# Narrower token tables in a fused attention and mixture-of-experts kernel, with the compact list read back from DRAM

## The chip, the cores and the metric

The kernel runs on one core of a Trainium2 chip. What counts is the device time of one execution in microseconds (us). Three runs of the kernel before took 1440.1, 1440.43 and 1440.45 us; the median is 1440.43.

## What is computed

Linear attention without a softmax feeds a mixture of experts that picks one expert per token; its rows feed a dense layer with a cosine.

```python
kv  = einsum('bhsd,bhse->bhde', k, v)            # 8 batches, 8 heads, 576 rows, 64 columns
out = einsum('bhsd,bhde->bhse', q, kv)
x   = out / sqrt(mean(out*out) + 1e-6) * g_norm   # as 4608 tokens of 512

e   = argmax(x @ w_gate)                          # one of 8 experts per token
y   = softmax(x @ w_gate)[e] * (relu(x @ w1[e]) @ w2[e])   # 512 -> 1024 -> 512

h   = y @ w_in                                    # 512 -> 2048
o   = (h * cos(h)) @ w_out                        # 2048 -> 512
```

Which token goes to which expert is known only on the chip, so the kernel keeps tables of token numbers.

## The kernel before

Everything is one function, `fused_kernel`, in which each engine's instructions stand in the order in which the Python code emits them; no scheduler moves them. An engine runs its own stream in order and waits on semaphores for the others.

**Attention and routing.** For each of the 8 batches TensorE makes `kv` (`emit_kv`), transposes q (`emit_qT`) and multiplies (`emit_out`), five row blocks `j` per batch. The VectorE work of the batch before is a generator, `route(b)`, from which `pump` takes three steps at a time between the TensorE calls: norms, logits, the expert's one-hot `esel`, the token's rank within its expert `rsel`. The rank is split into a row `cc` (rank modulo 128) and a column `aa` (expert times 36, plus rank divided by 128). For each row block, `emit_hot` (L513) builds two one-hot matrices on VectorE, `oc` (128 columns) and `oa` (288 columns, 36 per expert, times the token's number), and `emit_list` (L523) adds `oc^T @ oa` into the PSUM tile `lst`: 40 matmuls in all, two batches behind the attention. The result, `ids[p, e, t]`, holds the number of the token of rank 128 t + p of expert e. Experts are taken in order of their counts (`emit_order`); `emit_idx(r, ...)` selects the first 6 of the 36 columns of the r-th of them into `idx`, by which `gather` fetches token rows (GpSimd's indirect DMA).

**First layer of experts (moe1).** For each rank r of 8, `emit_f1` runs eight blocks c in one or two halves, and `emit_f2` four blocks in two halves, every product as three fp32r passes. `emit_f1` writes to one of three PSUM buffers, which ScalarE (L291) and VectorE (L292) empty; `emit_f2` and the transposes `emit_xT` of the next expert's rows share four PSUM buffers, and a transposed block is emptied by ScalarE (L272) and VectorE (L273). Between them stand, in this order, the split of one weight block into two parts (`next_split`, ScalarE with GpSimd L208 or VectorE L220), one step of the conversion of the dense layer's float64 weights (`prep`: VectorE L878 to L894, ScalarE L897 and L899, GpSimd L900 and L901), steps of `tables`, and `emit_clist`.

**Tables.** `tables` is a generator of VectorE operations, taken two steps per block of `emit_f1` and one per half of `emit_f2`. It makes the remaining `idx`, the counts, the first output column `basei` of each expert, the overflow counts `ovi`, and then for every token its position in the compact output: three times a product over 128x320 (L786) and its sum (L790), then `posq`, `posc`, `posa` (L795 to L806).

**The compact list.** `emit_clist` (L823) builds one-hots from those positions on VectorE (L835, L838) and adds them by matmul (L829) into the PSUM tile `clist`, one of 40 row blocks per half of `emit_f2` from r = 1 on. L1022 converts it into `ctok`, by which the dense layer's rows are scattered to the output (L1104).

**Overflow.** `emit_overflow` (L958) reads the overflow counts into registers of all engines (L960) and branches. No instruction behind that branch is in the trace.

**Dense layer (moe2).** Nine groups of 512 tokens by 16 blocks. Its weights come from the DRAM copy `wsp` by DMAs on GpSimd's queue (`load_m2`, L911).

SyncE issues the DMAs of q, k, v, of the attention rows `xs`, of the expert weights (L198, L213), of the raw dense weights and of the rows `ys` (L917), all in program order.

```python
def emit_list(b, j):
    oc, oa = tl.pop(("oh", b, j))
    nc.tensor.matmul(lst[:, 0:E * LT], lhsT=oc, rhs=oa, ...)
...
for u in range(2 * KD):
    if r > 0 or u % 2:
        emit_f2(r, u // 2, u % 2)
    next_split()
    prep()
    next(tabs, None)
    if r > 0:
        emit_clist()
    if r + 1 < E and u < ntile[r + 1]:
        emit_xT(r + 1, u)
```

Of the kernel before, what the change touches and what calls it, by code (L numbers as in the profile page):

```python
# [20 lines left out]
GATHER = 6  # L21
# [11 lines left out]
def fused_kernel(  # L33
# [43 lines left out]
    slots = dram.tile([(E + 1) * NT, 1], I32, name="slots")  # L77
    wsp = dram.tile([2 * C2, P, 2, 512], F32, name="wsp")
# [41 lines left out]
    def load_q(b):  # L120
        if b < B:
            load_rows(q[b], QT[b % 2])

# [10 lines left out]
    iota_a = const.tile([P, E * LT], F32, name="iota_a")  # L134
    nc.gpsimd.iota(iota_a, pattern=[[1, E * LT]], base=-E * LT, channel_multiplier=0,
                   allow_small_or_imprecise_dtypes=True)
    iota_b = const.tile([P, LT], F32, name="iota_b")
    nc.gpsimd.iota(iota_b, pattern=[[1, LT]], base=0, channel_multiplier=0,
# [44 lines left out]
    rsel = const.tile([P, B, NJ], F32, name="rsel")  # L183
    esel = const.tile([P, B, NJ, E], BF16, name="esel")
# [211 lines left out]
    def route(b):  # L396
# [39 lines left out]
        fm = sm([P, NJ], "fm")  # L436
        V.tensor_reduce(out=fm, in_=cd, axis=AX.X, op=ALU.min)
        tl["fm", b] = fm
# [34 lines left out]
        while ("rk", b) not in tl:  # L473
# [39 lines left out]
    def emit_hot(b, j):  # L513
# [4 lines left out]
        oa = late.tile([P, E * LT], F32R, tag="oa", name="oa", bufs=3)  # L518
# [64 lines left out]
    idx = const.tile([P, E, GATHER], I32, name="idx")  # L583

    def emit_idx(r, tab, sm=sm, n=GATHER):
# [3 lines left out]
        u = sm([P, GATHER], "iu")  # L589
# [5 lines left out]
    lst3 = lst[:, 0:E * LT].rearrange("p (e t) -> p e t", e=E)  # L595
    ids = const.tile([P, E, LT], F32, name="ids")
# [135 lines left out]
    basei = const.tile([P, E], I32, name="basei")  # L732
    ovi = const.tile([P, 2 * E + 1], I32, name="ovi")
    posc = const.tile([P, B * NJ], F32, name="posc")
    posa = const.tile([P, B * NJ], F32, name="posa")

    def tables(sm):
        V = nc.vector
        BT = B * NJ
# [6 lines left out]
        cols = sel.rearrange("p r e -> p e r")  # L746
# [27 lines left out]
        V.tensor_tensor(out=bov, in0=bov, in1=basef, op=ALU.subtract)  # L774
        V.tensor_tensor(out=bov, in0=bov, in1=capr, op=ALU.subtract)
        yield
# [3 lines left out]
        picks = []  # L780
        for n, vec in (("be", basef), ("de", bov), ("ce", capr)):
            ve = sm([P, E], n)
            rows(ve, cols, vec)
            yield
            t2 = sm([P, BT, E], "t2")
            V.tensor_tensor(out=t2, in0=esel.rearrange("p b j x -> p (b j) x"),  # L786
                            in1=ve[:, None, :].to_broadcast([P, BT, E]), op=ALU.mult)
            yield
            pk = sm([P, BT], "p" + n)
            V.tensor_reduce(out=pk, in_=t2, axis=AX.X, op=ALU.add)  # L790
            picks.append(pk)
            yield
        be, de, ce = picks
        rs = rsel.rearrange("p b j -> p (b j)")
        V.tensor_tensor(out=ce, in0=rs, in1=ce, op=ALU.is_ge)  # L795
        V.tensor_tensor(out=de, in0=de, in1=ce, op=ALU.mult)
        yield
# [25 lines left out]
    def emit_clist():  # L823
        i = len(hot2)
        if i > B * NJ + 1:
            return
# [346 lines left out]
```

## Time and profile before

| | us |
|---|---|
| median of three runs | 1440.43 |
| profiled execution, first to last instruction (span) | 1435.0 |
| what lies around the span (the difference of the two) | 5.4 |
| TensorE (PE) busy | 1370.3 (95%) |
| VectorE (DVE) busy | 976.2 (68%) |
| ScalarE (ACT) busy | 620.1 (43%) |
| GpSimd (POOL) busy | 389.5 (27%) |

The profile page gives no time of the profiled execution but its span. Attention lies at about 0 to 140 us, the first expert and the tables at 140 to 240, the rest of moe1 up to 632, the dense layer from 637 to the end. An engine's busy share is no measure of what bounds it; the waits of TensorE, and what ended each, say more. PEld is TensorE's weight load. A bracket in a timeline row, [4.00 <-DVE xreg L273], says how long the engine was idle before that row and which instruction released it.

### The profile page before, as it was taken

Reading aid. Unit: us, or ns where it says so; the run is one execution under the profiler, and the core shown is the slowest. Engines: PE = TensorE matmul, PEld = TensorE weight load, DVE = VectorE, ACT = ScalarE, POOL = GpSimd, SP = SyncE. Lnnn points to the kernel's source line nnn. Section 1 sums busy time; section 2 is a strip of 40 time slices with the busy share of each in tenths; the row PEclk is TensorE's granted clock in tenths of the full one; section 3 lists DMA queues with packets and bytes.
Section 4 is the critical chain, followed back from the end, with each engine's and each line's share of the span. In section 5 each row is a group of like instructions: output and inputs, shape, how many; then the busy total and the mean of one; then the engine's idle time right before and its main releaser. Section 6 shows DMA issues by size and latency. Waiting matters only on the chain.

```text
span 1435.0 us, 21374 instructions
## 1 busy us (share of the span) xinstructions
PE 1370.3 (95%) x8046; PEld 1208.8 (84%) x8046; DVE 976.2 (68%) x1720; ACT 620.1 (43%) x1195; POOL 389.5 (27%) x416
## 2 busy tenths in 40 slices
PE   6996798999999999989999999999999999999998
PEld 5885797999999999988888888888888888888886
DVE  2898868888888996316666666666666666665665
ACT  4886233444444444424434333443333433434333
POOL 1345534547456565220111101111011110011101
PEclk9998998999999999999999999999999999999999
DMA  9984355657676675774200001010000100000000
GB/s 316 340 295 136 129 151 170 213 186 219 201 220 209 196 240 167 221 223 148 88 30 23 22 16 30 30 30 30 8 23 30 30 30 15 16 30 1 30 0 30
DMA packets 137232, 162.22 MB, mean 113 GB/s; under 512 B 9428, under 2 KB 115924, under 8 KB 136096
## 3 DMA queue, kind: packets, MB, share of 16 engines
q1 hardware_dynamic: 111904, 97.54, 22.0%
q0 software_dynamic: 15296, 53.21, 10.9%
q10 hardware_dynamic: 9920, 10.03, 2.1%
q8 instruction: 65, 1.06, 0.3%
q14 instruction: 47, 0.39, 0.1%
HBM read 115.08 MB, written 45.66 MB: 112 GB/s over the span
## 4 chain that ended last, share of the span: by engine, by line
issue 32%; PE 18%; POOL 4%; DVE 1%; POOLq 0%; ACT 0%; DVEq 0%
PE gp L1046 9%; PE acc L1093 9%; POOL xreg L925 2%; POOL out_dram L1104 2%; DVE ra L1062 0%; DVE ra L1064 0%; DVE ni L1060 0%; POOL spare L1111 0%; POOLq L1168 0%; ACT ra L1067 0%; POOLq L925 0%; ACT ra L1066 0%; DVE ra L1074 0%; ACT gg L1075 0%; POOLq L1104 0%
## 5 line engine op out<-in xcount | busy, mean ns | idle before, releaser
L1046 PE MATMUL gp<-xreg,wA 128*128 128x512 f32 x1728 | 418.3, 392 | 5.2 <-ACTq L960 5.2
L1093 PE MATMUL acc<-wB,gg 128*128 128x512 f32 x1728 | 418.6, 391 | 0.1
L1046 PEld LDWEIGHTS gp<-xreg,wA 128*128 128x128 f32 x1728 | 325.9, 189 | 75.3 <-ACTq L960 5.5
L1093 PEld LDWEIGHTS acc<-wB,gg 128*128 128x128 f32 x1728 | 324.3, 188 | 70.8 <-DVE gg L1081 0.5
L1066 ACT ACTIVATE ra<-ra 128x512 f32<-128x512 f32 (+1 forms) x147 | 91.7, 623 | 380.6 <-DVE ra L1064 380.6
L289 PE MATMUL hp<-xreg,wA 128*128 128x352 f32 (+7 forms) x1536 | 226.1, 307 | 11.3 <-DVE wB L292 10.7
L289 PEld LDWEIGHTS hp<-xreg,wA 128*128 128x128 f32 x1536 | 219.0, 191 | 16.1 <-DVE wB L292 15.3
L302 PE MATMUL yp<-wB,wA 128*128 128x352 f32 (+7 forms) x1536 | 228.5, 307 | 4.1 <-DVE xreg L273 4.0
L302 PEld LDWEIGHTS yp<-wB,wA 128*128 128x128 f32 x1536 | 218.2, 190 | 4.6 <-DVE xreg L273 4.1
L1060 DVE TENSOR_SCALAR ni<-gp 128x512 int32<-128x512 f32 (+1 forms) x147 | 100.0, 680 | 170.3 <-PE gp L1046 170.3
L1074 DVE TENSOR_TENSOR ra<-gp,ra 128x512 f32<-128x512 f32 (+1 forms) x147 | 100.0, 680 | 114.8 <-ACT ra L1067 114.7
L925 POOL TENSOR_TENSOR xreg<-yst,xreg 128x512 fp32r<-128x512 f32 x32 | 41.5, 1296 | 367.3 <-ACT xreg L923 367.3
L1075 ACT ACTIVATE gg<-ra 128x512 fp32r<-128x512 f32 (+1 forms) x147 | 91.7, 624 | 92.8 <-DVE ra L1074 92.4
L1104 POOL DMA_INDIRECT out_dram<-oo,ctok x36 | 35.7, 993 | 331.3 <-DVE oo L1103 323.5
L1067 ACT ACTIVATE ra<-ra,half_pi 128x512 f32<-128x512 f32 (+1 forms) x147 | 105.1, 715 | 4.8
L1064 DVE SCALAR_TENSOR_TENSOR ra<-ni,ra 128x512 f32<-128x512 int32 (+1 forms) x147 | 100.1, 681 | 5.1
L208 POOL TENSOR_TENSOR wA<-w1s,wA 128x512 fp32r<-128x512 f32 x64 | 85.4, 1339 | 65.1 <-ACT wA L207 64.5
L1062 DVE SCALAR_TENSOR_TENSOR ra<-ni,gp 128x512 f32<-128x512 int32 (+1 forms) x147 | 99.5, 677 | 5.0
L1081 DVE TENSOR_TENSOR gg<-ra,gg 128x512 fp32r<-128x512 f32 (+1 forms) x147 | 98.9, 674 | 0.2 <-ACT gg L1075 0.2
L292 DVE SCALAR_TENSOR_TENSOR wB<-hp,wB 128x352 fp32r<-128x352 f32 (+7 forms) x128 | 57.7, 469 | 51.0 <-ACT wB L291 50.8
L291 ACT ACTIVATE wB<-hp 128x352 fp32r<-128x352 f32 (+7 forms) x128 | 52.6, 422 | 84.1 <-PE hp L289 83.7
L309 ACT ACTIVATE yo<-yp 128x352 f32<-128x352 f32 (+7 forms) x64 | 27.1, 423 | 89.7 <-PE yp L302 71.2
(188 smaller groups left out, 1308.9 us busy)
## 6 DMA issues: line engine op xcount, KB each, us to landing
w1s<-in_moe_w_dram SPq DMA_DIRECT2D x64, 256.0 KB, 4.4
w2s<-in_moe_w_dram SPq DMA_DIRECT2D x64, 256.0 KB, 3.7
wsp<-cd POOLq DMA_DIRECT2D x32, 512.0 KB, 4.0
yst<-ys SPq DMA_DIRECT2D x36, 256.0 KB, 2.6
xs<-xo SPq DMA_DIRECT2D x16, 512.0 KB, 4.3
raww<-in_moe_w_in_dram SPq DMA_DIRECT2D x16, 512.0 KB, 5.1
raww<-in_moe_w_out_dram SPq DMA_DIRECT2D x16, 512.0 KB, 5.2
wA<-wsp POOLq DMA_DIRECT2D x16, 512.0 KB, 5.2
```

Of the source, the lines that this page charges most:

```text
L289: nc.tensor.matmul(ps, lhsT=wv[:, a, kk, :], rhs=xT[:, b, kk, sl], start=(i == 0 and kk == 0), stop=(i == 2 and kk == KD - 1))
L302: nc.tensor.matmul(ps, lhsT=wv[:, a, kk % 4, :], rhs=hT[:, kk, b, sl], start=(n == 0), stop=(n == 3 * C1 - 1))
L1046: nc.tensor.matmul(ps, lhsT=wv[:, a, kk, :], rhs=yv[:, b, kk, :], start=(n == 0), stop=(n == 3 * KD - 1))
L1060: nc.vector.tensor_scalar(out=ni[:, h], in0=ps[:, h], scalar1=INV_2PI, scalar2=None, op0=ALU.mult)
L1062: nc.vector.scalar_tensor_tensor(out=ra[:, h], in0=ni[:, h], scalar=-PI2_HI, in1=ps[:, h], op0=ALU.mult, op1=ALU.add)
L1064: nc.vector.scalar_tensor_tensor(out=ra[:, h], in0=ni[:, h], scalar=-PI2_LO, in1=ra[:, h], op0=ALU.mult, op1=ALU.add)
L1066: nc.scalar.activation(ra[:, h], ra[:, h], AF.Abs)
L1067: nc.scalar.activation(ra[:, h], ra[:, h], AF.Sin, scale=-1.0, bias=half_pi)
L1074: nc.vector.tensor_tensor(out=ra[:, h], in0=ps[:, h], in1=ra[:, h], op=ALU.mult)
L1075: nc.scalar.activation(gg[:, 0, h], ra[:, h], AF.Copy)
L1081: nc.vector.tensor_tensor(out=gg[:, 1, h], in0=ra[:, h], in1=gg[:, 0, h], op=ALU.subtract)
L1093: nc.tensor.matmul(acc[g][t], lhsT=gg[:, a, t * P:(t + 1) * P], rhs=wv[:, b, :], start=(c == 0 and n == 0), stop=(c == C2 - 1 and n == 2))
```

## The change

Three parts.

1. The list's one-hot `oa`, the PSUM tile `lst` and `ids` have 6 columns per expert (48 in all) in place of 36 (288). A token of rank 768 or more gets a column outside the table: `route` has two more VectorE operations per batch, `qf` and an addition to `aa`.
2. `tables` loses the step between `ovi` and the remaining `idx`, and all that follows them (L780 to L806). Instead, `emit_idx` keeps its sums in `idf`, TensorE transposes it once (128x48 to 48x128, tile `idp`), and VectorE converts that into `idT`.
3. `emit_clist`, its 40 pairs of one-hots and 40 matmuls go. SyncE copies the 6 rows of `idT` of each expert into a DRAM list `cid` at that expert's first column, in the order of the experts, so that each copy overwrites the tail of the one before; after the branch one DMA reads `ctok` back from `cid`: 128 partitions by 36 single numbers of 4 bytes. SyncE therefore also loads `basei` into a register for seven experts. The code behind the overflow branch is rewritten to fit.

```diff
+    cid = dram.tile([2 * NT + P, 1], I32, name="cid")
...
-    iota_a = const.tile([P, E * LT], F32, name="iota_a")
+    iota_a = const.tile([P, E * GATHER], F32, name="iota_a")
...
+        qf = sm([P, NJ], "qf")
-        V.scalar_tensor_tensor(out=aa, in0=tl["fm", b], scalar=float(LT), in1=qi,
+        V.scalar_tensor_tensor(out=aa, in0=fm, scalar=float(GATHER), in1=qi,
                                op0=ALU.mult, op1=ALU.add)
+        V.tensor_scalar(out=qf, in0=qi, scalar1=float(GATHER), scalar2=float(NT),
+                        op0=ALU.is_ge, op1=ALU.mult)
...
+        V.tensor_tensor(out=aa, in0=aa, in1=qf, op=ALU.add)
...
-        oa = late.tile([P, E * LT], F32R, tag="oa", name="oa", bufs=3)
+        oa = late.tile([P, E * GATHER], F32R, tag="oa", name="oa", bufs=3)
...
-        nc.tensor.matmul(lst[:, 0:E * LT], lhsT=oc, rhs=oa,
+        nc.tensor.matmul(lst[:, 0:E * GATHER], lhsT=oc, rhs=oa,
...
-        u = sm([P, GATHER], "iu")
+        u = idf[:, r]
...
-        for n, vec in (("be", basef), ("de", bov), ("ce", capr)):
-            ve = sm([P, E], n)
-            rows(ve, cols, vec)
-            yield
-            t2 = sm([P, BT, E], "t2")
-            V.tensor_tensor(out=t2, in0=esel.rearrange("p b j x -> p (b j) x"),
-                            in1=ve[:, None, :].to_broadcast([P, BT, E]), op=ALU.mult)
-            yield
-            pk = sm([P, BT], "p" + n)
-            V.tensor_reduce(out=pk, in_=t2, axis=AX.X, op=ALU.add)
...
-        V.scalar_tensor_tensor(out=posc, in0=posq, scalar=-float(P), in1=be,
-                               op0=ALU.mult, op1=ALU.add)
-        V.tensor_copy(posa, posq)
+        ps = ps_a("idp")[0:E * GATHER, 0:P]
+        nc.tensor.transpose(ps, idf.rearrange("p e t -> p (e t)"), ident)
+        V.tensor_scalar(out=idT, in0=ps, scalar1=float(MID), scalar2=None, op0=ALU.add)
...
+    def copy_ids(r):
+        nc.sync.dma_start(
+            cid[bass.ds(bv[r], GATHER * P), :].rearrange("(t c) o -> t (c o)", c=P),
+            idT[r * GATHER:(r + 1) * GATHER, :])
...
-                bv[r] = nc.values_load(basei[0:1, r:r + 1], engines=(ET.Activation,), min_val=0,
-                                       max_val=NT)
+                bv[r] = nc.values_load(basei[0:1, r:r + 1], engines=(ET.Activation, ET.SP),
+                                       min_val=0, max_val=NT)
...
-            if r > 0:
-                emit_clist()
+            if r > 0 and u == 3:
+                if r == 1:
+                    copy_ids(0)
+                copy_ids(r)
...
-    while len(hot2) <= B * NJ + 1:
-        emit_clist()
-    nc.vector.tensor_scalar(out=ctok, in0=clist[:, 0:LT], scalar1=float(MID), scalar2=None, op0=ALU.add)
+    nc.sync.dma_start(ctok, cid[0:NT, :].rearrange("(t p) o -> p (t o)", p=P))
```

VectorE, second layer of the first expert, before: xreg is the next expert's transposed block, raww and the numbered c tiles are the weight conversion, esel, de and pde the tables.

```order
L273 SCALAR_TENSOR_TENSOR xreg<-xTp,gv,xreg 128x4x128
L892 TENSOR_SCALAR c_2831<-raww 128x512
L894 SCALAR_TENSOR_TENSOR c_2831<-raww,c_2831 128x512
L786 TENSOR_TENSOR t_2906<-esel,de 128x320
L273 SCALAR_TENSOR_TENSOR xreg<-xTp,gv,xreg 128x4x128
L878 TENSOR_SCALAR c_2950<-raww 128x512
L881 TENSOR_SCALAR c_2952<-raww 128x512
L790 TENSOR_REDUCE pde<-t_2906 128x40
L273 SCALAR_TENSOR_TENSOR xreg<-xTp,gv,xreg 128x4x128
```

The same place of the changed kernel (its lines 272, 829, 832, 843 and 845 are 273, 878, 881, 892 and 894 of before):

```order
L272 SCALAR_TENSOR_TENSOR xreg<-xTp,gv,xreg 128x4x128
L843 TENSOR_SCALAR c_2832<-raww 128x512
L845 SCALAR_TENSOR_TENSOR c_2832<-raww,c_2832 128x512
L272 SCALAR_TENSOR_TENSOR xreg<-xTp,gv,xreg 128x4x128
L829 TENSOR_SCALAR c_2943<-raww 128x512
L832 TENSOR_SCALAR c_2945<-raww 128x512
L272 SCALAR_TENSOR_TENSOR xreg<-xTp,gv,xreg 128x4x128
```

The two table operations between the blocks are gone; nothing else moved there.

TensorE, first layer of the first expert, changed kernel (hp is a block of `emit_f1`, idp the new transpose):

```order
L301 MATMUL yp<-wB_2155,wA_2156 128x352 x24
L288 MATMUL hp<-xreg,wA_169 128x352 x72
L779 MATMUL idp<-ident,idf 48x128
L288 MATMUL hp<-xreg,wA_169 128x352 x24
L269 MATMUL xTp<-ident,xg 128x128 x4
```

Before, all 96 of these hp matmuls stood in one piece; now the transpose stands ahead of the last 24.

SyncE, second layer of the second expert, changed kernel: the first two copies into `cid` stand between loads of expert weights.

```order
L808 DMA raww<-in_moe_w_in_dram 128x4x128
L197 ISA
L197 DMA w1s<-in_moe_w_dram 128x4x128
L941 DMA cid<-idT 6x128
L941 REGISTER_ALU
L941 DMA cid<-idT 6x128
L197 ISA
L197 DMA w1s<-in_moe_w_dram 128x4x128
```

Loads that followed each other before now have these copies between them, which are queued on the same engine.

## Rows read from the trace of the kernel before

**Rows 1.** Stretches: busy us (x instructions) of PE, PEld, DVE, ACT, POOL, PEclk, DMA share, GB/s.
```profile
60.00:80.00 20.00, 19.22 (x256) 17.21 (x257) 18.99 (x57) 17.22 (x52) 10.95 (x12) 1.00 1.06 360
140.00:160.00 20.00, 14.55 (x82) 13.63 (x81) 18.40 (x40) 9.45 (x23) 12.07 (x12) 0.83 0.43 139
220.00:240.00 20.00, 13.70 (x67) 13.42 (x68) 18.82 (x32) 5.67 (x11) 8.82 (x8) 0.81 0.51 163
```
**Rows 2.** Waits of PE, 0 to 240 us: us in total, times, longest.
```profile
PE lst L525 <- DVE oa L519: 19.6, 16, 5.4
PE yp L302 <- DVE xreg L273: 4.0, 1, 4.0
PE hp L289 <- DVE wB L292: 3.0, 1, 3.0
```
**Rows 3.** Groups by line: shapes, count, busy us, mean ns, idle before.
```profile
L838 DVE TENSOR_SCALAR oa<-iota_b,posa,idv 128x36 fp32r<-128x36 f32 x40 | 27.3, 681 | 0.0
...
L835 DVE TENSOR_SCALAR oc<-iota_c,posc 128x128 fp32r<-128x128 f32 x40 | 26.6, 666 | 0.0
```
**Rows 4.** Lines 519 and 838: duration ns min/median/max, first and last start us.
```profile
L519 DVE TENSOR_SCALAR oa<-iota_a,aa,idv x40: 413/424/2379, 51.2 to 172.2; 128x288 fp32r<-128x288 f32 x40
...
L838 DVE TENSOR_SCALAR oa<-iota_b,posa,idv x40: 289/298/2040, 272.1 to 532.4; 128x36 fp32r<-128x36 f32 x40
```
**Rows 5.** Timeline of PE in attention: start us, us, operation.
```profile
44.04 0.60 PE L369 MATMUL qTp<-ident,qc 128*128 128x128 f32 x4
44.48 1.15 PE L380 MATMUL op<-kv,qT 128*128 128x144 f32 x8
...
54.67 0.60 PE L369 MATMUL qTp<-ident,qc 128*128 128x128 f32 x4
...
55.24 1.14 PE L380 MATMUL op<-kv,qT 128*128 128x144 f32 x8
```
**Rows 6.** Timeline of PE in the second expert, around a compact-list matmul.
```profile
288.82 0.18 PE L829 MATMUL clist<-oa,oc 128*128 128x36 f32 x1
288.85 3.94 PE L302 MATMUL yp<-wB,wA 128*128 128x336 f32 x24
```
**Rows 7.** Timeline of DVE, 143 to 238 us.
```profile
143.55 6.78 DVE L484 TENSOR_SCALAR qi<-rsel 128x5 int32<-128x5 f32 x1
150.36 0.17 DVE L488 SCALAR_TENSOR_TENSOR aa<-fm,qi 128x5 f32<-128x5 f32 x1
...
202.41 0.24 DVE L590 TENSOR_REDUCE iu<-it 128x6 f32<-128x48 f32 x1
...
213.14 4.25 DVE L786 TENSOR_TENSOR t<-esel,de 128x320 f32<-128x320 bf16 x1
...
217.97 2.82 DVE L878 TENSOR_SCALAR c<-raww 128x512 int32<-128x512 int32 x1
...
222.51 0.73 DVE L273 SCALAR_TENSOR_TENSOR xreg<-xTp,gv,xreg 128x512 fp32r<-128x512 f32 x1
```
**Rows 8.** Timeline of POOL beside two of these.
```profile
149.04 1.25 POOL L220 TENSOR_TENSOR wA<-w2s,wA 128x512 fp32r<-128x512 f32 x1
...
215.72 1.31 POOL L901 TENSOR_TENSOR cd<-c,c 128x512 fp32r<-128x512 f32 x1
```
**Rows 9.** Timeline of PE, 189 to 265 us.
```profile
189.63 15.38 PE L289 MATMUL hp<-xreg,wA 128*128 128x352 f32 x96
...
223.30 6.63 PE L302 MATMUL yp<-wB,wA 128*128 128x352 f32 x24 [4.00 <-DVE xreg L273]
...
238.47 26.07 PE L289 MATMUL hp<-xreg,wA 128*128 128x336 f32 x156 [3.00 <-DVE wB L292]
```
**Rows 10.** The page, part 3: SyncE's DMA queue (packets, MB, share of 16 engines).
```profile
q1 hardware_dynamic: 111904, 97.54, 22.0%
```
**Rows 11.** Timeline of POOL at the start of moe2.
```profile
643.71 0.53 POOL L911 DMA_DIRECT2D wB<-wsp  x1 [2.25 <-DMA wB<-wsp]
```
**Rows 12.** Timeline of PE at the same place.
```profile
647.78 2.88 PE L1093 MATMUL acc<-wB,gg 128*128 128x512 f32 x12
```

More of the change, by code (lines that the diff above doesn't have):

```diff
@@ L183, in fused_kernel @@
     rsel = const.tile([P, B, NJ], F32, name="rsel")
+    fsel = const.tile([P, B, NJ], F32, name="fsel")
     esel = const.tile([P, B, NJ, E], BF16, name="esel")
@@ L435, in route @@
         yield
-        fm = sm([P, NJ], "fm")
+        fm = fsel[:, b]
         V.tensor_reduce(out=fm, in_=cd, axis=AX.X, op=ALU.min)
-        tl["fm", b] = fm
         ex = sm([P, NJ, E], "ex")
@@ L583, in fused_kernel @@
     idx = const.tile([P, E, GATHER], I32, name="idx")
+    idf = const.tile([P, E, GATHER], F32, name="idf")
+    idT = const.tile([E * GATHER, P], I32, name="idT")
     def emit_idx(r, tab, sm=sm, n=GATHER):
@@ L593, in emit_idx @@
                                 scalar2=None, op0=ALU.add)
-    lst3 = lst[:, 0:E * LT].rearrange("p (e t) -> p e t", e=E)
-    ids = const.tile([P, E, LT], F32, name="ids")
+    lst3 = lst[:, 0:E * GATHER].rearrange("p (e t) -> p e t", e=E)
+    ids = const.tile([P, E, GATHER], F32, name="ids")
     chain = iter(())
@@ L928, in overflow_tile @@
     def overflow_tile(r, first, it):
+        row = expert(r) * NT + it + CAPS[r]
         ix = wk.tile([P, 1], I32, tag="ox", name="ox")
-        nc.sync.dma_start(ix, slots[bass.ds(expert(r) * NT + it + CAPS[r], P), :])
+        nc.sync.dma_start(ix, slots[bass.ds(row, P), :])
+        nc.sync.dma_start(cid[bass.ds(first + it, P), :], slots[bass.ds(row, P), :])
         xr = gp.tile([P, DM], F32, tag="xg", name="xr")
@@ L960, in emit_overflow @@
         with tc.If(any_ov > 0):
-            lt = cpool.tile([P, E, LT], I32, tag="cd", name="lt", bufs=2)
-            nc.vector.tensor_scalar(out=lt, in0=ids, scalar1=float(MID), scalar2=None, op0=ALU.add)
-            nc.sync.dma_start(
-                slots[0:E * NT, :].rearrange("(e t p) o -> p e (t o)", e=E, p=P), lt)
-            nc.sync.dma_start(slots[E * NT:E * NT + P, :], lt[:, 0, 0:1])
+            ns = (E + 1) * NT // P
+            z = cpool.tile([P, ns], I32, tag="cd", name="z", bufs=2)
+            nc.vector.memset(z, 0)
+            nc.sync.dma_start(slots.rearrange("(p n) o -> p (n o)", p=P), z)
+            sl = cpool.tile([P, 2, B, NJ], I32, tag="cd", name="sl", bufs=2)
+            sf = cpool.tile([P, B, NJ], F32, tag="c2", name="sf")
+            nc.vector.scalar_tensor_tensor(out=sf, in0=fsel, scalar=float(NT), in1=rsel,
+                                           op0=ALU.mult, op1=ALU.add)
+            nc.vector.tensor_scalar(out=sl[:, 0], in0=sf, scalar1=float(E * NT), scalar2=None,
+                                    op0=ALU.add)
+            nc.vector.tensor_scalar(out=sl[:, 1], in0=idv, scalar1=float(MID), scalar2=None,
+                                    op0=ALU.add)
+            for b in range(B):
+                for j in range(NJ):
+                    w = P if j < 4 else 64
+                    nc.gpsimd.indirect_dma_start(
+                        out=slots[:, :], in_=sl[0:w, 1, b, j:j + 1], in_offset=None,
+                        out_offset=bass.IndirectOffsetOnAxis(ap=sl[0:w, 0, b, j:j + 1], axis=0))
             for r in range(E):
```

47 lines of the change are left out of this document (1 added, 46 removed).

## The prediction

> **What bounds the kernel now.** I read the profile by stretches first, then the waits of TensorE (PE) within the stretches that the change touches, then the timelines around the longest of these waits. From 60 to 80 us PE is busy 19.2 of 20 us and VectorE (DVE) 19.0: attention is held by PE, with DVE close behind [rows 1]. [...] The waits say whom PE waits for: 19.6 us for the list's one-hots, 4.0 for an emptied transpose, 3.0 for an emptied block of the first layer, all on DVE [rows 2].
>
> Why DVE is late there shows in its timeline beside GpSimd's (POOL). L484, five columns wide, takes 6.78 us and ends as POOL's run of operations does, at 150.3. L786, a table product, takes 4.25 us and ends at 217.4, 0.4 us after POOL's L901 [rows 7, 8]. So some DVE operations stand still while POOL computes, and what is queued behind them stands too: the emptied transpose L273 comes only at 222.5, and PE, which needs that buffer, idles 4.00 us [rows 7, 9]. The 24 matmuls after that idle time take 6.63 us, against 3.94 for 24 elsewhere [rows 6, 9]. So an idle stretch costs twice, the second time by the clock.
>
> **The change part by part.**
>
> *Narrower lists.* 40 list matmuls go from 288 to 48 columns. In attention the step from a transpose to the next block takes 0.44 us without a list matmul (44.04 to 44.48) and 0.57 with one (54.67 to 55.24): it costs 0.13 [rows 5]. A 36-column matmul moves its successor by 0.03 (288.82 to 288.85), which I take for 48 columns too [rows 6]. So 0.10 is saved for each of the 20 that stand where PE is the bound (lists of batches 0 to 3): 2.0 us. Against it stand two new small DVE operations per batch ahead of the first one-hot, 0.17 us each by L488 [rows 7]; the shorter one-hot gives 0.13 back (424 against 298 ns [rows 4]), so the first list matmul of each of four batches waits about 0.2 longer: 0.8. The net is -1.2. The other 20 stand where DVE is the bound. Each saves 0.126 us of DVE, 2.5 in all; the new operations take 4 times 0.34 = 1.4. Some 0.5 comes from the two copies into `ids`, which shrink alike. That is -1.6, a part of which POOL's runs will swallow, as they did with L484: I take -1.5. Lists: **-2.7**, between 0 (all swallowed) and -5 (20 times 0.13, plus 2.5 on DVE).
>
> *The new transpose.* In the first layer of the first expert PE runs 96 matmuls without a gap, 15.38 us from 189.63 [rows 9]. The transpose stands after 72 of them, that is at about 201.2. It needs the sum of the last expert's indices, and DVE gets to that only behind the block that PE has just finished: its third-last sum ends at about 202.65 in the trace (202.41 plus 0.24), in the place where now the last one stands [rows 7]. PE thus waits 1.5 us where it did not wait, plus some 0.2 for the transpose itself: **+1.7**, between 1 and 4 (a collision with POOL in front of it, as large as L878's 2.82 [rows 7]). Behind it wait the 24 matmuls and everything of PE after them.
>
> *The position tables.* Between 204 and 238 us DVE is relieved of three products, three sums, six small operations with sums, and the last seven: raw some 7 us, and 3.8 more in which L786 stood still. PE lost there 4.00 and 3.00 us of waits, 2.7 by the clock (6.63 against 3.94), and about 1.0 more in the 156 matmuls that took 26.07, against 25.0 at the rate of 15.38 for 96, scaled to 336 columns [rows 6, 9]: 10.7 us in all, the most that can come back. Without L786 the two transposes behind it can be emptied as soon as ScalarE has done its half, so the wait of 4.0 and its clock loss should go. But the conversion's operations stay, and L878 alone stood still for 2.82 us [rows 7]; when the next wait comes, at the start of the second expert, DVE is late by these next. I keep 2.7 of 10.7 as lost: **-8.0**, between -2 and -10.7.
>
> *The compact list.* 40 matmuls at 0.03 go [rows 6]: **-1.2**. The 80 one-hots were 53.9 us of DVE [rows 3], yet no wait of PE in that stretch is for them; the blocks that PE waits for are emptied in `emit_f1`, half an expert later. This part I cost at 0; what hides the one-hots is the slack of the three PSUM buffers. POOL meets fewer operations of DVE, which I leave at 0 too.
>
> *The copies.* Eight copies of 6 rows of 512 bytes and seven register loads stand on SyncE among weight loads. The second copy waits for the first to land, some microseconds, with the weight loads of the third expert behind it. The weights of an expert are asked for three staging buffers ahead, and PE never waited for one in moe1: 0. The last DMA reads 4608 single numbers. The scatters that need them come after 16 blocks of twice 12 matmuls, 2.88 us for 12 [rows 12], some 90 us, so its own time, even 30 us, is covered. What it shares is the 16 DMA engines with the dense layer's weights (a rival, below): 0, between 0 and +12.
>
> The sum is -2.7 + 1.7 - 8.0 - 1.2 = -10.2 against the profiled execution, whose span is 1435.0 with 5.4 around it, just the median of 1440.43. I take **1430 us**.
>
> **The rivals.**
>
> *A. The collisions stay.* The table operations leave, but POOL's runs hit the next DVE operation of the same kind: L878 comes at once behind, and L273 is queued behind that. For it: five columns were held for 6.78 us, so the size of what stands still does not matter [rows 7]. Against: two operations of four between the transposes go, and L786 was the longest. Half of the 4.00, half of the 2.7 and 2 of the 3.00 would stay, and the part gives -5 in place of -8, the lists -1: 1440.4 - 1 + 1.7 - 5 - 1.2 = 1435.
>
> *B. All of it comes back.* The whole 10.7, the lists' 5, 1.2 less 1.7: -15.2, **1425**. For it: DVE has room once the tables are gone. Against: L878, which stays, stands still behind POOL without any table's help [rows 7].
>
> *C. The small read starves the dense layer.* SyncE's queue took 22.0% of 16 engines' span for 111904 packets: 0.22 x 16 x 1435 / 111904 = 45 ns each, of some 870 bytes [rows 10]. 4608 packets over 16 engines are 288 each, 13 us at that price; a packet of 4 bytes may cost less, or more, if the price is not one of bytes. The read is issued as the branch ends, just when the dense layer's weights are. The first second-layer weight has landed by 643.7, and PE needs it at 647.8: 4.1 us of slack [rows 11, 12]. If all 288 pieces pass ahead of it, PE waits 13 - 4.1 = 8.9, and 2.7 more by the clock: +11.6, 1441.6, no change. At 60 ns a piece (17.3 us) it is +15.9: 1446, slower. The point from which it decides is where 288 pieces less 4.1, plus 2.7, exceed the 10.2 gained: 41 ns, without taking turns. Against: with turns, piece by piece, the first three weight loads (24 packets an engine) are held up by 24 x 45 ns = 1.1 us, inside the slack. The trace has both queues at work at once in moe1, with no wait of PE for weights.
>
> [...]
>
> **How the numbers follow.** Forecast (1426 to 1434): 0.56. A (1434 to 1440): 0.20, of which a third is within 0.2% of no change. B (1420 to 1426): 0.11. C: 0.09, of which two thirds are slower. What is left, 0.04, I count as no change. I call 0.2%, 2.9 us, about what a measurement of this kernel can tell from none. Faster: 0.56 + 0.11 + two thirds of 0.20 = 0.81; slower 0.06; the same 0.13. The range of 1422 to 1439 leaves out C, the end of A and the far end of B, some 0.18.
>
> **What would show it.** Right: PE's wait for L273 and its slow 24 matmuls near 220 us are gone, the second expert's second layer begins some 8 us earlier than at 264.5 (238.47 + 26.07 [rows 9]), and PE's list waits fall by two or three us of 19.6. A new wait of PE, about 1.5 us, stands before the transpose. No gap opens at the first second-layer matmul of moe2. The dense layer takes as long as before. Wrong: if the second expert begins no earlier, DVE still stands still behind POOL (A). If the dense layer's first weights land after PE asks for them, C holds. If moe1 beyond 265 us shortens by more than 3 us, the one-hots were on the path after all, and I missed why.

## The result, and the profile after

The changed kernel takes 1422.07 us (median of four; 1421.02 to 1425.06), the kernel before 1440.44. The ratio is 0.9867, 95% interval 0.9852 to 0.9883: 18.4 us less, and in a later run of five 20.4 less. The direction was forecast, the size was not: 1430, with 1422 as the lower end.

One number ahead of the sum was wrong. The profiled execution of before had a span of 1435.0, and I put 5.4 us "around the span". Every execution since, of both kernels, has 1.8 to 2.5 there. So the execution shown was a quick one, of some 1437: twelve later ones of the same kernel took 1439.3 to 1446.2. So two executions of each kernel stand side by side here, the second pair from the runs `e0_before` and `e4_after`. The stages are cut at the starts of PE's groups in the timeline.

| stage (us) | before | before again | changed | changed again |
|---|---|---|---|---|
| to the first block of the first expert | 139.67 | 140.64 | 134.59 | 135.06 |
| to the second half of its first layer | 49.96 | 51.78 | 50.63 | 51.06 |
| to the second expert's second layer | 74.75 | 75.54 | 71.58 | 71.76 |
| to the last expert's second layer | 343.40 | 345.79 | 338.28 | 338.74 |
| to the first second-layer matmul of moe2 | 40.00 | 40.32 | 38.70 | 39.69 |
| to the end | 787.22 | 787.23 | 786.02 | 785.69 |
| span | 1435.0 | 1441.3 | 1419.8 | 1422.0 |

The gain sits in attention (5.1 to 5.6), in the tables' stretch (3.2 to 3.8) and in the rest of moe1 (5.1 to 7.1). The forecast had put 2.7, 6.3 (8.0 less 1.7) and 1.2 there. A further 1.2 to 1.5 us sits in the dense layer, which the change does not touch and which was forecast to take as long as before: its matmuls follow each other every 223 to 238 ns in place of 223 to 242 (from 800 to 1300 us). Why is open; the layer's time differs in the same way between other runs below.

The page of the changed kernel, its first part:

```profile
span 1419.8 us, 21248 instructions
...
PE 1362.0 (96%) x8007; PEld 1203.9 (85%) x8007; DVE 937.2 (66%) x1635; ACT 620.0 (44%) x1195; POOL 391.2 (28%) x415
```

DVE lost 39 us of 976, PE 8 of 1370. The same three stretches as [rows 1], with the same columns:

```profile
60.00:80.00 20.00, 18.97 (x271) 17.45 (x270) 18.94 (x64) 17.67 (x51) 10.11 (x11) 1.00 1.04 359
140.00:160.00 20.00, 12.67 (x68) 11.56 (x67) 19.45 (x40) 6.07 (x13) 12.38 (x12) 0.83 0.40 125
220.00:240.00 20.00, 16.08 (x91) 15.25 (x91) 17.04 (x25) 8.11 (x17) 9.53 (x8) 0.91 0.55 178
```

From 140 to 160 DVE still holds PE, and the granted clock is 0.83 as before; from 220 to 240 PE is busy 16.1 in place of 13.7, and the clock rose from 0.81 to 0.91. PE's waits up to 240 us, to be read against [rows 2]:

```profile
PE lst L528 <- DVE oa L522: 17.8, 16, 5.5
...
PE hp L288 <- DVE wB L291: 2.8, 3, 1.3
...
PE idp L779 <- DVE idf L595: 1.6, 1, 1.6
```

The wait of 4.0 for an emptied transpose is gone, the new transpose waits 1.6, the lists' wait fell by 1.8 only, and the wait for the first layer's emptied block is 2.8 where it was 3.0. PE's timeline around the tables shows where they went, against [rows 9]:

```profile
198.38 0.27 PE L779 MATMUL idp<-ident,idf 128*48 128x128 f32 x1 [1.59 <-DVE idf L595]
...
216.86 4.07 PE L301 MATMUL yp<-wB,wA 128*128 128x352 f32 x24
...
224.58 5.50 PE L288 MATMUL hp<-xreg,wA 128*128 128x336 f32 x24 [1.80 <-ACT xreg L271]
231.37 3.96 PE L288 MATMUL hp<-xreg,wA 128*128 128x336 f32 x24 [1.29 <-DVE wB L291]
```

The 24 matmuls that took 6.63, at a granted clock of 0.58 in the mean from 223.3 to 229.9, now take 4.07, at 1.00 from 216.8 to 221. But the second expert's first layer meets a new wait, 1.80 for a block that ScalarE empties, and the 24 matmuls behind it run 5.50, at 0.69 from 224.6 to 230.1 (3.95 in the second execution, after the same wait). The wait for VectorE's block, one of 3.00 before, stands there still: 1.29 and 0.82 here, 2.87 at once in the second execution. Together they keep 3.9 and 4.7 us of what the tables' stretch had lost.

The last read of the compact list, from the view of its tile (the last columns are its first and last start), from the list of DMAs (KB, us to landing), and PE's timeline at the dense layer:

```profile
L993 SPq DMA_DIRECT2D ctok<-cid x1: 422/422/422, 622.9 to 622.9; - x1
```

```profile
ctok<-cid SPq DMA_DIRECT2D x1, 18.0 KB, 23.6
```

```profile
633.78 2.88 PE L1064 MATMUL acc<-wB,gg 128*128 128x512 f32 x12
```

The 4608 pieces are issued at 622.9 and land 23.6 us later, at 646.5. PE's first second-layer matmul stands at 633.78 without a wait, and the first scatter at 720: the dense weights passed beside the pieces. In every 2 us from 628 to 642, 223 to 247 packets of 4 bytes start, and 206 to 219 of the weights' queue.

### The profile page after: what moved, and what is told of

Read it like the earlier page. It is cut to its first block, busy times and chain, and to the rows that moved or that the text cites. A ratio compares the mean times of both kernels' runs of the same rounds, so it can differ in the third digit from the quotient of the medians.

```text
span 1419.8 us, 21248 instructions
## 1 busy us (share of the span) xinstructions
PE 1362.0 (96%) x8007; PEld 1203.9 (85%) x8007; DVE 937.2 (66%) x1635; ACT 620.0 (44%) x1195; POOL 391.2 (28%) x415
## 4 chain that ended last, share of the span: by engine, by line
issue 44%; PE 6%; POOL 5%; DVE 1%; POOLq 0%; ACT 0%; DVEq 0%
PE gp L1017 3%; PE acc L1064 3%; POOL xreg L876 3%; POOL out_dram L1075 2%; POOL spare L1082 0%; DVE ni L1031 0%; DVE ra L1033 0%; DVE ra L1035 0%; POOLq L876 0%; POOLq L1139 0%; ACT ra L1038 0%; ACT ra L1037 0%; POOLq L1075 0%; DVE ra L1045 0%; ACT gg L1046 0%
## 5 line engine op out<-in xcount | busy, mean ns | idle before, releaser
L288 PE MATMUL hp<-xreg,wA 128*128 128x352 f32 (+7 forms) x1536 | 225.4, 306 | 12.8 <-DVE wB L291 10.1
L207 POOL TENSOR_TENSOR wA<-w1s,wA 128x512 fp32r<-128x512 f32 x64 | 85.8, 1348 | 61.0 <-ACT wA L206 60.4
L291 DVE SCALAR_TENSOR_TENSOR wB<-hp,wB 128x352 fp32r<-128x352 f32 (+7 forms) x128 | 57.8, 470 | 62.0 <-ACT wB L290 61.9
```

The source lines that it names most:

```text
L288: nc.tensor.matmul(ps, lhsT=wv[:, a, kk, :], rhs=xT[:, b, kk, sl], start=(i == 0 and kk == 0), stop=(i == 2 and kk == KD - 1))
```

## The experiments

Each median stands against that of the kernel before, timed beside it (1442.2 to 1443.3). An interval is that of the ratio. The changed kernel's own difference is 20.4; it was timed beside `e5`, `e6` and `e7` alone, so that every other comparison with it goes by way of the kernel before.

| run | what it is | median | ratio, 95% | against before |
|---|---|---|---|---|
| e0_before | kernel before | 1442.34 | 0.9999 (0.9988 to 1.0011) | 0.0 |
| e4_after | changed kernel | 1422.86 | 0.9862 (0.9843 to 0.9881) | -20.4 |
| e1_lists | before, lists narrow | 1436.81 | 0.9956 (0.9939 to 0.9972) | -5.6 |
| e2_tables_clist | changed, lists wide | 1430.23 | 0.9913 (0.9899 to 0.9927) | -12.2 |
| e7_tables_back | changed, table work back | 1430.59 | 0.9910 (0.9892 to 0.9928) | -12.7 |
| e3_clist_back | changed, compact-list work back | 1433.48 | 0.9932 (0.9910 to 0.9954) | -8.9 |
| e5_mm_only | changed, its 40 matmuls back | 1427.12 | 0.9895 (0.9876 to 0.9913) | -16.2 |
| e6_hot_only | changed, its 80 one-hots back | 1432.07 | 0.9920 (0.9902 to 0.9938) | -11.2 |
| e15_hot_two | the 80, two columns wide | 1426.41 | 0.9897 (0.9880 to 0.9914) | -16.0 |
| e9_hot_thin | the 80, one column wide | 1421.35 | 0.9860 (0.9838 to 0.9881) | -21.0 |
| e16_hot_one | the same again | 1423.32 | 0.9875 (0.9858 to 0.9891) | -19.1 |
| e10_hot_nopool | e6, GpSimd's products out | 1410.24 | 0.9784 (0.9765 to 0.9803) | -32.1 |
| e11_after_nopool | changed, the same out | 1410.34 | 0.9783 (0.9765 to 0.9801) | -32.0 |
| e12_after_conv | changed, new conversion | 1408.15 | 0.9762 (0.9740 to 0.9784) | -34.1 |
| e13_before_conv | before, new conversion | 1422.29 | 0.9868 (0.9844 to 0.9891) | -19.9 |
| e14_conv_idp | e12, transpose later | 1408.47 | 0.9765 (0.9741 to 0.9788) | -33.7 |
| e8_lists_moved | changed, lists and transpose moved | 1424.31 | 0.9880 (0.9861 to 0.9900) | -18.1 |

**The kernel before again.** No edit.

> The kernel before, unchanged, to see the span beside the time. If 5.4 us around the span is what this kernel has, its span is about 1435.0 at a time of 1440.4 and the change took 3.6 us outside the span. If the profiled execution was a quicker one than the three timed, what lies around is 1.8 us as in every run of the changed kernel, and the span belongs to a time of about 1436.8.

Twelve executions lie 1.9 to 2.4 us above their spans, which run from 1437.4 to 1444.3. The 5.4 was the difference between one quick execution's span and other executions' median.

**The parts alone.** The changed kernel itself; the first part of the change alone on the kernel before; the changed kernel with lists of 36 columns (`GATHER` back to `LT` in `oa`, `lst` and `ids`, without `qf`); and with the table work behind its transpose:

```diff
         V.tensor_scalar(out=idT, in0=ps, scalar1=float(MID), scalar2=None, op0=ALU.add)
+        picks = []
+        for n, vec in (("be", basef), ("de", bov), ("ce", capr)):
...
+        V.tensor_copy(posa, posq)
```

> The changed kernel itself, on the same chip as the parts. By the ratio measured so far, 0.987, about 1423 us where the kernel before takes 1442.4; its spread is expected to be narrower (some 4 us) than that of the run with the compact list put back (10 us), if collisions of the one-hots make that spread.

> Part 1 alone: lists of 6 columns per expert; tables, compact list and no copies as before. The prediction's term: -2.7 us against before, about 1437.7. What the trace after the change shows at the first matmul of moe1 (134.59 against 139.67): -5.1 us, about 1435.3, with the five list matmuls behind each other near 120 us quicker by about 2.9 of these.

> Parts 2 and 3 alone: lists of 36 columns as before. The prediction's terms (tables -8.0, transpose +1.7, compact list -1.2): -7.5 against before, about 1433, and 2.7 slower than the full change. The theory that the one-hots of the compact list were on the path (some 5 us in moe1 beyond the second expert) and the lists worth 5.1: 5.1 slower than the full change, about 1427.

> The changed kernel with the operations of the position tables put back behind the new transpose, their result unused. The prediction's term for them: +8.0 against the changed kernel. What the stretch from the second half of the first expert to the second layer of the second expert shows (74.75 us before, 71.58 after, with the transpose's wait of 1.6 in the latter): +3.2 to +4.8.

The lists are worth 5.6 us on the kernel before, and 8.2 on top of the rest (20.4 less 12.2), not 2.7. The table work costs 7.7 where 8.0 was forecast, more than I read from the stretch of the two traces. In its profile that stretch is 5.7 longer than the changed kernel's (77.45 against 71.76); less the transpose's 1.6 that is 4.1, near what the table of stages shows (3.2 to 3.8). The other 2 us lie spread over the other stages. In all executions with wide lists the first block of the first expert starts at 139.7 to 140.9 (four), with narrow ones, apart from `e8`, at 134.0 to 138.0 (fourteen). Up to the twentieth list matmul, where PE is the bound, the gain is what was forecast: 51.49 us from the first to the twentieth before, 50.27 after, 1.2 less. The rest comes behind it: some 1.4 us at the two list matmuls near 113 us, and 2.3 (8.87 us from the first to the last before, 6.46 after) where five follow each other. DVE's last one-hot of those five and GpSimd's run beside it, before:

```profile
126.90 1.06 DVE L516 TENSOR_SCALAR oc<-iota_c,cc 128x128 fp32r<-128x128 f32 x1
127.88 2.38 DVE L519 TENSOR_SCALAR oa<-iota_a,aa,idv 128x288 fp32r<-128x288 f32 x1
...
123.71 5.16 POOL L463 TENSOR_TENSOR xo<-raw,inv 128x512 f32<-128x512 f32 x5
128.84 1.25 POOL L208 TENSOR_TENSOR wA<-w1s,wA 128x512 fp32r<-128x512 f32 x1
```

and after:

```profile
122.69 1.12 DVE L519 TENSOR_SCALAR oc<-iota_c,cc 128x128 fp32r<-128x128 f32 x1
123.73 1.04 DVE L522 TENSOR_SCALAR oa<-iota_a,aa,idv 128x48 fp32r<-128x48 f32 x1
...
120.69 5.03 POOL L461 TENSOR_TENSOR xo<-raw,inv 128x512 f32<-128x512 f32 x5
125.69 1.25 POOL L207 TENSOR_TENSOR wA<-w1s,wA 128x512 fp32r<-128x512 f32 x1
```

In that run of five products of some 1.03 us each, a one-hot takes 1.04 to 1.16 us in place of 0.3 or 0.4 (one before took 0.47, one after 0.53). Before, the last one missed the end of the run and stood through the next operation too, to 130.26, 0.2 behind L208's end; after, it was through at 124.8, inside the run, and the operation behind it (L403, of the routing) stood 2.30 us instead. PE's list no longer waited for the longest of these.

**The compact list, whole and in halves.** The work stands where it stood, its result unused. For the matmuls alone each takes the same pair `hot0`, made once ahead of moe1; for the one-hots alone the matmul is left out of `emit_clist`.

```diff
             next(tabs, None)
+            if r > 0:
+                emit_clist()
```

> The changed kernel with the 80 one-hots and the 40 matmuls of the compact list put back in their place, their result unused; the copies and the last read stay. By the prediction (40 matmuls at 0.03, the one-hots free): +1.2 against the changed kernel, about 1423.3. Matmuls at 0.07 each and free one-hots: +2.8, about 1424.9. One-hots on the path, through what is emptied late behind them: +5, about 1427.

> The changed kernel with the 40 matmuls of the compact list alone put back, all from one pair of one-hots that is made once. The prediction's 0.03 each: +1.2 against the changed kernel. At 0.05 to 0.07 each, as the second-layer stretches of the trace differ (0.34 to 0.55 for eight): +2.0 to +2.8. If TensorE's order is what cost the 10 us of the whole list: +10.

> The changed kernel with the 80 one-hots of the compact list alone put back on VectorE, without the matmuls. The prediction's cost: 0. The theory that they delay the blocks which VectorE empties for TensorE at the start of each first layer: +6 to +8, with TensorE's wait for L291's block up from 7 to 10 us or more in moe1.

The whole costs 11.5 (20.4 less 8.9), the matmuls 4.2, the one-hots 9.2, of which some 1.4 lie in the dense layer (below); the whole's six times spread over 10.1 us, the changed kernel's five over 3.4. The matmuls' cost is in the second layers, where they stand: those of the second to the sixth expert take 0.43, 0.62, 0.95, 1.40 and 0.80 longer than in `e4_after`, 4.2 for 38 matmuls, 0.11 each and not 0.03 (0.08 without one wait of 1.1 for an emptied transpose among them). The one-hots' cost is elsewhere: those second layers grow by 0.0 in all, the first layers behind them by 1.65, 1.58, 1.13, 1.45 and 2.42, 8.2 together. PE's waits from 262 to 590 us, of the changed kernel and of the one with the one-hots:

```profile
PE hp L288 <- DVE wB L291: 7.4, 10, 1.3
```

```profile
PE hp L291 <- DVE wB L294: 14.6, 15, 2.3
```

It is the same wait, for the block that DVE empties, and it doubled. One of them, in the timelines of DVE, GpSimd and PE with the one-hots back:

```profile
285.32 2.82 DVE L808 TENSOR_SCALAR oa<-iota_b,fsel,idv 128x36 fp32r<-128x36 f32 x1
...
292.37 1.32 DVE L805 TENSOR_SCALAR oc<-iota_c,rsel 128x128 fp32r<-128x128 f32 x1
293.60 1.27 DVE L808 TENSOR_SCALAR oa<-iota_b,fsel,idv 128x36 fp32r<-128x36 f32 x1
294.79 0.87 DVE L294 SCALAR_TENSOR_TENSOR wB<-hp,wB 128x316 fp32r<-128x316 f32 x2
...
285.53 2.56 POOL L210 TENSOR_TENSOR wA<-w1s,wA 128x512 fp32r<-128x512 f32 x2
...
291.86 1.74 POOL L872 TENSOR_TENSOR cd<-c,c 128x512 fp32r<-128x512 f32 x1
293.56 1.26 POOL L873 TENSOR_TENSOR cd<-c,c 128x512 fp32r<-128x512 f32 x1
...
288.60 5.31 PE L291 MATMUL hp<-xreg,wA 128*128 128x316 f32 x36
295.32 4.87 PE L291 MATMUL hp<-xreg,wA 128*128 128x316 f32 x32 [1.40 <-DVE wB L294]
```

A one-hot of 36 columns takes 2.82 us and ends at 288.1 as GpSimd's L210 does; two more end at 293.7 and 294.9 with L872 and L873. In that run 26 of the 80 one-hots last more than half again their least time, and every one of the 26 ends within 0.1 us after an operation of GpSimd. In these second layers PE does not wait for DVE, so nothing showed DVE falling behind. At the border the first layer fills its three buffers in 5.3 us, and the first emptying comes only behind the queue, at 294.8: that is where PE pays.

**Length, number or kind.** The 80 one-hots with one and with two columns (`wk.tile([P, 1], ...)` and `iota_c[:, 0:1]`, the same with 2).

> As the run with the 80 one-hots alone put back, but each one column wide. If their own length is what cost 9.2 us (0.28 and 0.30 us each undisturbed, 23 us in all): with 0.15 us or so each, half of it or less, +4 against the changed kernel. If their number is, since each in turn stands still behind a GpSimd operation whatever its size: +7 to +9, with their mean duration still 0.6 us or so.

> The 80 one-hots alone put back, two columns wide each. At one column they cost nothing and lasted 0.20 and 0.26 us in the mean. If length is what counts, two columns cost nothing either and last as long. If one column is the exception (the operation takes another path and does not stand still), two columns are as dear as 36 and 128: mean 0.5 us or more, +6 to +9 against the changed kernel, about 1430.

> The same at one column once more, since the five times of the first run were 1421 four times and 1428 once: about 1421 to 1422, means of 0.20 and 0.26 us again.

The view of one line gives min/median/max ns of the 40 operations L808, at one, two and 36 columns (the second run with one column, then the two others):

```profile
L808 DVE TENSOR_SCALAR oa<-iota_b,fsel,idv x40: 255/263/267, 264.7 to 521.8; 128x1 fp32r<-128x1 f32 x40
```

```profile
L808 DVE TENSOR_SCALAR oa<-iota_b,fsel,idv x40: 275/282/1951, 262.0 to 523.5; 128x2 fp32r<-128x2 f32 x40
```

```profile
L808 DVE TENSOR_SCALAR oa<-iota_b,fsel,idv x40: 290/298/3175, 265.0 to 529.2; 128x36 fp32r<-128x36 f32 x40
```

At one column no operation stands still, though 48 and 51 of the 80 run beside one of GpSimd's; at two, with a median only 19 ns longer, they do, up to 1951 ns, and all 30 that last over half a microsecond end with an operation of GpSimd. Against the changed kernel the totals are -0.6 and +1.3 at one column, 4.4 at two, 9.2 at full width. But they cannot be read as they stand, because the dense layer, where none of these operations is, differs between the runs. The stretch is the one from the second expert's second layer to the last expert's, where the one-hots stand; VectorE's time is the sum of their 80 durations.

| run | VectorE's time for the 80 | stretch | dense layer | total against the changed kernel | the same without the dense layer |
|---|---|---|---|---|---|
| changed kernel, two executions | 0 | 338.3, 338.7 | 786.0, 785.7 | 0 | 0 |
| one column, `e9`, `e16` | 18.7, 18.7 | 341.7, 340.2 | 782.1, 782.1 | -0.6, +1.3 | 3, 5 |
| two columns, `e15` | 55.4 | 343.5 | 782.1 | +4.4 | 8 |
| full width, `e6` | 57.8 | 347.1 | 787.3 | +9.2 | 8 |

With one and two columns all matmuls of the dense layer follow each other every 225 to 228 ns; why they do there and not elsewhere is open. Without that layer one column is not free, and two columns cost some 8, within the 6 to 9 of the second theory. The last column goes by one profile per run, and is good to some 2 us. Firmer is the difference between two columns and one, timed beside each other and with equal dense layers: 3.1 in the medians (1426.41 less 1423.32), 3.2 in the stretch. So the number of the operations is one part of the price, and the standing still, which comes with the second column, is another of at least 3; whether the full width adds to it is not shown (3.7 by the stretch, nothing by the last column).

**GpSimd out of the conversion.** Of the conversion of the dense weights, GpSimd's two products per step go: first left out (`e10`, `e11`), then made unnecessary. In the rewrite VectorE's mask keeps the top 11 bits of the mantissa, so that the high part needs no product, and the low part is one VectorE operation:

```diff
-            nc.vector.tensor_scalar(out=sc, in0=hi, scalar1=3, scalar2=0x3F800000, ...)
+            nc.vector.tensor_scalar(out=sc, in0=hi, scalar1=3, scalar2=0x3FFFF000, ...)
-            nc.vector.scalar_tensor_tensor(out=ef, in0=ex, scalar=float(0x38100000), ...)
+            nc.vector.scalar_tensor_tensor(out=d[:, 0], in0=ex, scalar=float(0x38100000), ...)
-            nc.vector.tensor_scalar(out=ex, in0=hi, scalar1=9, scalar2=0x7FF, ...)
+            nc.vector.tensor_scalar(out=ef, in0=d[:, 0].bitcast(I32), scalar1=-0x800000, ...)
...
-            nc.scalar.activation(mf, ex, AF.Copy, scale=2.0 ** -11, bias=1.0)
-            nc.scalar.activation(ml, sc, AF.Copy, scale=2.0 ** -35)
-            nc.gpsimd.tensor_tensor(out=d[:, 0], in0=mf, in1=ef, op=ALU.mult)
-            nc.gpsimd.tensor_tensor(out=d[:, 1], in0=ml, in1=ef, op=ALU.mult)
+            nc.vector.scalar_tensor_tensor(out=d[:, 1], in0=sc, scalar=2.0 ** -35,
+                                           in1=ef.bitcast(F32), op0=ALU.mult, op1=ALU.mult)
```

> The 80 one-hots put back, and GpSimd's two products per step of the weight conversion left out (ScalarE writes the two parts unscaled, so the dense layer works on other numbers). To be read against the same without the one-hots. If GpSimd's runs make the one-hots dear: they cost 4 us or less there, and their mean duration falls from 0.72 to below 0.5 us. If VectorE is simply full: 9 us as before.

> The changed kernel with the same two products of GpSimd left out (the dense layer works on other numbers), without the one-hots. If GpSimd's runs also set TensorE's waits for L291's block that stay in the changed kernel (7.4 us in moe1): 3 to 6 us faster than the changed kernel. If not: the same.

> The changed kernel with the weight conversion rewritten so that GpSimd computes nothing in it: VectorE makes both parts itself (eight operations per step in place of seven, ScalarE and GpSimd none). If GpSimd's products are what makes VectorE's operations long, the eighth operation is more than paid for: 8 to 12 us faster than the changed kernel, about 1412. If VectorE is simply full, the 32 further operations of 0.69 us cost: about 1425 to 1430.

> The kernel before with the same rewritten conversion. If standing still behind GpSimd is why the parts of the change gave more than their plain lengths, the change is worth less here: lists 5, tables 3 to 5, matmuls 4, one-hots 0 to 2, less 1.6 for the transpose, 11 to 14 us between this run and the changed kernel with that conversion, against 20.4 between the two kernels. If not: 20 us here too.

Without GpSimd's products the same 80 one-hots cost nothing (1410.24 against 1410.34; in their stretch 329.38 against 329.34), and take 35.2 us of VectorE in place of 57.8. The changed kernel itself is 11.6 us faster, twice what was expected. With the rewrite it takes 1408.15, 13.7 less than without by the two differences from the kernel before, though VectorE has one operation more per step: this version is faster than both kernels. The rewrite takes two operations per step from ScalarE as well; `e11`, which keeps these, is the run that shows GpSimd's part alone. The view of the line L843 of the conversion, in the changed kernel and with the rewrite (where it is an operation of the same form):

```profile
L843 DVE TENSOR_SCALAR c<-raww x32: 414/1516/3073, 210.4 to 547.2; 128x512 int32<-128x512 int32 x32
```

```profile
L843 DVE TENSOR_SCALAR c<-raww x32: 410/419/727, 211.7 to 533.0; 128x512 int32<-128x512 int32 x32
```

Its median falls from 1516 to 419 ns, near its least time; the waits of 7.4 us for the emptied block do not appear at all any more from 262 to 608 us. With that conversion the change is worth 14.1 (1422.29 less 1408.15) in place of 20.4, the upper end of what was expected. In the profiles moe1's share of it fell from 5.1 and 7.1 to 3.0 (330.73 less 327.69), about what the matmuls alone cost. So some 6 us of the gain by the totals (each time is good to some 2), 2 to 5 by the stretches in which the conversion runs, were VectorE's standing still behind these two products. How much of the other 14 is standing still behind GpSimd's other work, `xo` in attention and the halves of the weight split (L207), stays open: that work was not taken away.

**The waits that stayed.** The transpose two steps later, alone on the rewrite; and on the changed kernel together with list matmuls in later places and five buffers for the one-hots.

```diff
+        yield
+        yield
         ps = ps_a("idp")[0:E * GATHER, 0:P]
```
```diff
-    for j in range(NJ):
-        emit_list(B - 3, j)
     att_a.close()
...
         emit_out(B - 1, j)
+        emit_list(B - 3, j)
...
-        if 2 <= c < 2 + NJ:
-            emit_list(B - 2, c - 2)
+        if 3 <= c < 3 + NJ:
+            emit_list(B - 2, c - 3)
```

> The changed kernel with the rewritten conversion and the new transpose two steps of the generator later. Its wait of 1.6 us on VectorE goes: 1 to 2 us faster than the run with the conversion alone. If the wait only moves to the first layer of the second expert, the same.

> A version meant to be faster than both: the changed kernel with the new transpose two steps of the generator later (its wait of 1.6 us on VectorE should go), the five list matmuls that stood behind each other near 120 us spread over the last batch's row blocks (they wait 5.5 us in all), and the sixth batch's lists one block of the first layer later (one wait of 5.5 us at 146 us), with five buffers for the one-hots in place of three. If TensorE's order is what these waits cost: -6 to -9 against the changed kernel, about 1415. If VectorE behind GpSimd bounds that stretch whatever TensorE's order is: -1.6 from the transpose alone, about 1421.

Neither helped. In `e14` the wait of 1.59, which the rewrite alone still has, is gone, and the time is the same (1408.47 against 1408.15, within the intervals). In `e8` the lists' waits of PE fell from 17.1 to 10.0 us, and others came for them, 14.6 in place of 11.4 for the emptied block and 7.5 for blocks of attention that ScalarE empties (L384), which stood at 0.2 in the first profile of the changed kernel; the first block of the first expert starts at 136.94, not earlier. So the order of TensorE's work is not what these waits cost. That VectorE behind GpSimd sets the pace there fits its 19.45 busy us of 20 from 140 to 160 in the changed kernel, but this run does not show it.

## Why the prediction was wrong

- **The frame.** The "5.4 around it" came of a quick execution beside slower ones; true is about 1.9. It hid some 3.5 us of the change's effect in the traces that I compared.
- **Narrower lists, -2.7.** The half where PE is the bound came out as worked (1.2). The step that failed is "Each saves 0.126 us of DVE", and that GpSimd's runs would swallow a part of it: measured -5.6 alone. In the rows above the one-hot that stood still lasted to the end of one of GpSimd's operations (127.88 to 130.26, and L208 ended at 130.09), and the earlier start, near 120 us, saved that whole operation of 1.25 us, not 0.126. What gave the 1.4 us near 113 us stays open.
- **The new transpose, +1.7.** The wait is there as forecast, 1.59 us at 198.38. Taking it away, on the rewritten conversion, changed nothing that can be measured, so as a term it was worth less there.
- **The position tables, -8.0.** Measured 7.7, in part by luck. L273's wait and its slow matmuls went as said. But more than the 2.7 kept as lost stayed, 3.9 and 4.7 (the waits of 1.80, 1.29 and 0.82, and of 1.80 and 2.87), and 2 us of the 7.7 came outside the stretch. One sum is wrong too: 15.38 for 96, scaled to 156 matmuls and to 336 columns, gives 23.9 and not 25.0, so that 11.9 and not 10.7 was the most that could come back.
- **The compact list, -1.2.** This is the term that was mis-sized most: put back, the whole costs 11.5. "40 matmuls at 0.03" measured 0.11 each; one row (288.82 to 288.85) was taken for all, and the stretches of eight show more. The one-hots are the step that failed: "This part I cost at 0; what hides the one-hots is the slack of the three PSUM buffers" measured 9.2, some 8 without the dense layer. That PE shows no wait for the one-hots in that stretch was true and proved nothing: that DVE fell behind there was paid for at the next place where PE needs it (PE's wait for the block that DVE empties went from 7.4 to 14.6 us, the first layers behind grew by 8.2), and the three buffers were full after 5.3 us. The rows were at hand: their medians (298 ns for L838 [rows 4]) against their means (681 ns [rows 3]) said that they stood still more than they worked.
- **Copies and the last read, 0, and rival C.** Nothing waited for them. C needed the dense weights to stand behind the pieces; both passed side by side, 223 to 247 pieces and 206 to 219 packets of the weights' queue in every 2 us from 628 to 642, and PE does not wait at 633.78. The point from which C decides is 40 ns by its own sum, not 41.
- **Rivals A and B, and the signs.** B's time (1425) was nearest, by luck: it returned the tables' and the lists' whole cost, and left the one-hots at 0. The second expert's second layer began 7.6 us earlier than at 264.5, about the 8 that was to show the forecast right, but attention gave 5.1 of these, where 2.7 was forecast. The sign that would refute me was on record: moe1 beyond 265 us shortening by more than 3 us. It shortened by 5.1, and by 7.1 in the second pair.

The parts do not add up exactly: 5.6, 7.7 and 11.5 less 1.6 are 23.2 against 20.4. With medians good to some 2 us that is within what can be told; that they overlap on the same standing still is likely, but was not shown. Putting the compact list back is not quite its removal reversed, either: in the profile of `e3` the stretch from the second to the last expert's second layer takes 349.59, where the kernel before took 343.40 and 345.79. Some 1.2 to 1.5 us belong to the dense layer and to no part.

## What to carry to other kernels

An operation of an engine that nobody waits for is free only if that engine is on time at the next place where somebody does wait: the 80 one-hots, for which PE never waited in their stretch of the kernel before, cost 9.2 us when put back. Follow the engine's queue to there before costing an operation at nothing. Compare the mean of an operation with its median or least time: here a mean of 681 ns against a median of 298 [rows 3, 4], and a median of 1516 against a least time of 414, were operations standing still beside GpSimd's. Cost it at its mean, and ask what holds it up: that other work may be the cheaper thing to move (GpSimd's two products out: 11.6 us). Before a small difference is put down to an edit, check that stages which the edit does not touch kept their times; here the dense layer's were 782.1 to 787.3. One profiled execution has its own time, here 1435.0 beside spans of 1437.4 to 1444.3: cost a change against several spans.

## What the runs showed of the hardware

- Some of VectorE's one-hots, each made from one tensor in SBUF and scalars, stood still while GpSimd computed, at two columns (L808: 282 ns median, 1951 at most) and at 36 (298 median, 3175 at most), but none at one (267 at most of 40). All 26 long one-hots of `e6` end within 0.1 us after an operation of GpSimd, and all 30 of `e15` end with one. One instruction of GpSimd is not the limit: L484 stood 6.78 us [rows 7], while GpSimd's beside it took 1.25 [rows 8]. Why the single column never stood still is not shown.
- L272, which empties a transpose from PSUM beside one input in SBUF, took no part in this: 748 ns in the mean in the changed kernel (128x512, `e4_after`, 296 to 570 us) and 749 with GpSimd's products gone (`e12`).
- A matmul of 36 columns between long ones cost 0.06 (five second layers with the rewrite, 2.4 longer for 38 of them) to 0.11 us, two to four times what the next row's start suggested.
- The read of 4608 single numbers landed after 23.6 us, beside weight loads, and PE did not wait for those at 633.78.
- The same matmuls of the dense layer took 782.1 us in the three runs with one or two columns and 785.5 to 787.3 in all others; what decides it is open.
